# Two-queue filter loads, duplicated rows and one product on GpSimd in the first batch of a fused spectral-filter and MLP kernel

## The chip, the cores and the metric

The kernel runs on one core of one Trainium2 chip. The metric is the device time of one execution in microseconds (us), median of several. Engines are named as in the profile: PE is TensorE, DVE is VectorE, ACT is ScalarE, POOL is GpSimd, SP is SyncE. SP does little but issue transfers here. Moments such as "16.08" are us from the start of the profiled span.

## The reference

Each of 8 sequences of 3008 x 256 goes through a real FFT along the sequence, is multiplied by a complex filter and transformed back; then each of the 24064 tokens goes through a two-layer MLP with a gated activation.

```python
X = np.fft.rfft(x, axis=1)
F = (filt_r + 1j * filt_i)[None, :, :]
y = np.fft.irfft(X * F, n=x.shape[1], axis=1)
h = y.reshape(24064, 256) @ w_in                      # 256 x 2048
out = (h * (1.0 / (1.0 + np.exp(-beta * h)))) @ w_out  # 2048 x 256
```

## The kernel before

The MLP of one batch runs on PE for about 100 us, and the transform of the next batch is slipped between its matmuls by a fixed plan of steps. Only the first batch's transform stands alone, at the start, with the loads of the constants beside it. The change concerns that stretch.

The spectrum lies in six *units* of four rows each (24 rows, `KU = 4`). For each unit, PE makes a bank `sps`, DVE multiplies it by the real and by the imaginary filter (`fr_sb`, `fi_sb`: 128 partitions x 24 x 256 float32), and PE transforms the two products back. Both filters are needed on all 128 partitions, but the two halves hold the same values. So each is loaded to one half only, in a forward and a mirrored piece (the mirrored one reads its rows backwards, in packets of 1 KB), and POOL copies it to the other half ("spread").

```python
    def load_filters(k0, k1):
        n = k1 - k0
        for filt, dst, p0 in ((filt_r, fr_sb, M), (filt_i, fi_sb, 0)):
            for q0, off, sg in ((p0, k0, 1), (p0 + H, N1 - k0, -1)):
                src = AP(filt.tensor, filt.offset + off * D, [[N1 * D, H], [sg * D, n], [1, D]])
                nc.sync.dma_start(dst[q0 : q0 + H, k0:k1, :], src)
    # ... cut ...
    for u in range(NUN):
        load_filters(u * KU, (u + 1) * KU)      # 24 loads of 128 KB on SP's hardware queue
    # ... cut ...
    p0pool = rpool("p0pool", r_p0, bufs=2, **tw)
    def s2_0(u):
        ps = bank2([P, KU, D])
        # ... four matmuls into ps; pq[u, 0], pq[u, 1] = tiles of p0pool, two buffers each ...
        nc.vector.tensor_tensor(pq[u, 0][:], ps[:], fr_sb[:, ks, :], ALU.mult)
        nc.vector.scalar_tensor_tensor(pq[u, 1][:], ps[:], rot[:], fi_sb[:, ks, :], ALU.mult, ALU.mult)
    # ... unit(u): PE transforms pq[u, 0] and pq[u, 1] back, ACT empties the bank ...
    def spread(u):
        ks = slice(u * KU, (u + 1) * KU)
        nc.gpsimd.tensor_copy(fr_sb[:M, ks, :], fr_sb[M:, ks, :])
        nc.gpsimd.tensor_copy(fi_sb[M:, ks, :], fi_sb[:M, ks, :])
    # ... order on POOL: spread(0..3), win load, spread(4), win load, spread(5), x of batch 1 ...
```

Of the kernel before, what the change touches and what calls it, by code (L numbers as in the profile page):

```python
# [22 lines left out]
M = 64  # L23
# [13 lines left out]
def kernel(  # L37
# [48 lines left out]
    def load_filters(k0, k1):  # L86
        n = k1 - k0
        for filt, dst, p0 in ((filt_r, fr_sb, M), (filt_i, fi_sb, 0)):
            for q0, off, sg in ((p0, k0, 1), (p0 + H, N1 - k0, -1)):
                src = AP(filt.tensor, filt.offset + off * D, [[N1 * D, H], [sg * D, n], [1, D]])  # L90
                nc.sync.dma_start(dst[q0 : q0 + H, k0:k1, :], src)  # L91
# [49 lines left out]
    def iota(tile_, pattern, base=0, ch=0):  # L141
        nc.gpsimd.iota(tile_, pattern=pattern, base=base, channel_multiplier=ch)
# [42 lines left out]
    iota(vi[:, :, :H], [[1, NK], [N1, H]])  # L185
    load_x0(16, 24)
    iota(vi[:, :, H:], [[1, NK], [-N1, H]], base=N1 * (M - 1))
# [31 lines left out]
    v_i = shift_and("v_i", 5, 1)  # L219
    q_p = (affine("q0", q_i, -1.0, 1.0), affine("q1", q_i, 1.0, 0.0))  # L220

    def t2_half(hi):
        t = sq.tile([P, NK, H], I32, name="u", tag=f"u{hi}")
        nc.vector.tensor_scalar(  # L224
            t[:], vi[:, :, hi * H : (hi + 1) * H], ms[:], off[:], ALU.mult, ALU.add
        )
        fold(t[:])
        nc.scalar.activation(
            t2[:, :, hi * H : (hi + 1) * H], t[:], ACT.Sin, scale=TWO_PI / TURN
        )  # L230

    def t2_shift(hi):
        for c in range(2):
            d0, s0 = (0, M) if c == 0 else (M, 0)
            dst = t2[d0 : d0 + M, :, M + hi * H : M + (hi + 1) * H]
            src = t2[s0 : s0 + M, :, hi * H : (hi + 1) * H]
            if c == hi:
                nc.vector.tensor_scalar_mul(dst, src, -1.0)
            else:
                nc.vector.tensor_copy(dst, src)  # L240
# [26 lines left out]
    def spin(n, idle):  # L267
        for _ in range(n):
            nc.tensor.matmul(idle[:], lhsT=rest[:, :P], rhs=rest[:], start=True, stop=True)
# [41 lines left out]
    for u in range(NUN):  # L311
        load_filters(u * KU, (u + 1) * KU)
    gp = nc.gpsimd
    rot = affine("rot", v_i, 2.0, -1.0, gp)
# [3 lines left out]
    gp.tensor_tensor(beta_sb[:], tiny[:], beta_sb[:], ALU.add)  # L318
    s1_0(0, (False,))
    s1_0(1, (True,))  # L320
    spin(5, idle)
    t2_shift(0)
    t2_shift(1)
# [102 lines left out]
    def s2_0(u):  # L426
        ps = bank2([P, KU, D])
        for i in range(KU):
            k1 = u * KU + i
            nc.tensor.matmul(ps[:, i, :], lhsT=t2[:, k1, :], rhs=a0[:, k1, :], start=True, stop=True)  # L430
        ks = slice(u * KU, (u + 1) * KU)
        for c in range(2):
            pq[u, c] = p0pool.tile([P, KU, D], BF16, name="pq_t", tag=f"pq{c}")
        nc.vector.tensor_tensor(pq[u, 0][:], ps[:], fr_sb[:, ks, :], ALU.mult)
        nc.vector.scalar_tensor_tensor(
            pq[u, 1][:], ps[:], rot[:], fi_sb[:, ks, :], ALU.mult, ALU.mult
        )
# [45 lines left out]
    spread(4)  # L483
    load_win(4 * P, FF)
    spread(5)
    for g in range(4):
        load_x(1, g)
    load_wout(0)
    load_wout(WG)
    scale_wout(0)  # L490
    scale_wout(WG)
# [8 lines left out]
    s2_0(2)  # L500
    unit(1)
    a0_turn(4)
    s2_0(3)
    unit(2)
    s2_0(4)
    a0_turn(5)
    t3_part(2, True)
    t3_neg(2, True)
    unit(3)
    s2_0(5)  # L510
    idle = tpsum.tile([P, 512], F32, name="tps", tag="tps")
    spin(3, idle)
    unit(4)
# [158 lines left out]
    for b in range(1, B):  # L672
        o = first_step[b - 1]
        if b == 1:
            at(0, z_late, 1, 0)
            at(1, z_late, 1, 1)
            s1_steps(1, range(16), [1 + (2 * i + 1) // 3 for i in range(16)], False, (1, 4, 7, 10, 13))
            for i, r in enumerate((11, 12, 13, 14)):
                at(r, f_late, 1, i // 2, i % 2)
            for g in range(NG):  # L680
                at(o + 13, a2_load, 1, g)
# [147 lines left out]
```

## Time and profile before

| | before |
|---|---|
| time, median (range) | 782.4 us (781.73 to 782.9), 4 runs |
| first filter product / third unit's first product | 16.08 / 20.74 |
| last filter product ends | 30.61 |
| first MLP matmul | 33.84 |
| wait for batch 1's x | 0.84 at 36.61 |

The prediction below shows the waits of PE, the windows and the end of the first batch. The timeline of POOL (start, duration, engine, line, operation, in brackets the idle time before it and what ended that):

```profile
13.11 1.03 POOL L472 COPY fr_sb<-fr_sb 64x1024 f32<-64x1024 f32 x1 [0.98 <-DMA fr_sb<-in_filt_r_dram]
...
28.23 1.04 POOL L473 COPY fi_sb<-fi_sb 64x1024 f32<-64x1024 f32 x1
29.21 2.06 POOL L171 DMA_DIRECT2D xg<-in_x_dram  x4
```

Twelve copies of about 1.04 us, with two loads of `win` between them, fill most of POOL's time from 13 to 29 us, and x can be issued only behind them. The third unit's first product, in DVE's timeline, waits for nothing:

```profile
20.74 1.21 DVE L434 TENSOR_TENSOR pq_t<-sps,fr_sb 128x1024 bf16<-128x1024 f32 x1
```

Then the DMA issues (size of one, median us from issue to landing):

```profile
fr_sb<-in_filt_r_dram SPq DMA_DIRECT2D x12, 128.0 KB, 4.4
fi_sb<-in_filt_i_dram SPq DMA_DIRECT2D x12, 128.0 KB, 4.4
```

They go out on one queue, unit by unit, real and imaginary in turn, which is the order in which DVE needs them.

### The profile page before, as it was taken

Reading aid. Unit: us, or ns where it says so; the run is one execution under the profiler, and the core shown is the slowest. Engines: PE = TensorE matmul, PEld = TensorE weight load, DVE = VectorE, ACT = ScalarE, POOL = GpSimd, SP = SyncE. Lnnn points to the kernel's source line nnn. Section 1 sums busy time; section 2 is a strip of 40 time slices with the busy share of each in tenths; the row PEclk is TensorE's granted clock in tenths of the full one; section 3 lists DMA queues with packets and bytes.
Section 4 is the critical chain, followed back from the end, with each engine's and each line's share of the span. In section 5 each row is a group of like instructions: output and inputs, shape, how many; then the busy total and the mean of one; then the engine's idle time right before and its main releaser. Section 6 shows DMA issues by size and latency. Waiting matters only on the chain.

```text
span 780.2 us, 15154 instructions
## 1 busy us (share of the span) xinstructions
PE 764.1 (98%) x5956; PEld 544.0 (70%) x6051; DVE 446.0 (57%) x713; ACT 552.6 (71%) x814; POOL 151.4 (19%) x155
## 2 busy tenths in 40 slices
PE   8899999999999999999999999999999999999997
PEld 5677667766776667866678666776667776676665
DVE  7869754766556665566546665567655666321001
ACT  6767877676677766777667776677766777777776
POOL 6714400312012210122201322022200222000000
PEclk9999999999999999999999999999999999999999
DMA  9975585244913358042671417622164111500101
GB/s 185 233 213 116 147 209 155 70 108 115 252 42 80 103 116 242 29 113 71 152 207 45 119 48 181 176 75 69 48 189 135 48 48 49 156 28 28 55 28 55
DMA packets 84411, 88.51 MB, mean 113 GB/s; under 512 B 5788, under 2 KB 74652, under 8 KB 84340
## 3 DMA queue, kind: packets, MB, share of 16 engines
q1 hardware_dynamic: 79892, 73.81, 32.0%
q0 software_dynamic: 4304, 13.60, 10.5%
q8 instruction: 47, 0.77, 0.4%
q14 instruction: 24, 0.20, 0.1%
q10 hardware_dynamic: 144, 0.13, 0.0%
HBM read 54.47 MB, written 46.66 MB: 130 GB/s over the span
## 4 chain that ended last, share of the span: by engine, by line
PE 94%; DMA 2%; issue 1%; POOL 1%; DVE 1%; SPq 0%; ACT 0%; DVEq 0%; POOLq 0%
PE acc L788 43%; PE hps L770 39%; PE ps L561 3%; PE ps L629 3%; PE ps L607 3%; PE ps L577 2%; DMA xg<-in_x_dram 1%; DMA fi_sb<-in_filt_i_dram 1%; POOL fi_sb L473 0%; POOL fr_sb L472 0%; SPq L91 0%; PE ps L405 0%; PE tp L400 0%; DVE y L114 0%; DVE u L224 0%
## 5 line engine op out<-in xcount | busy, mean ns | idle before, releaser
L779 ACT ACTIVATE gT<-hps,beta_sb 128x512 bf16<-128x512 f32 x752 | 516.9, 687 | 213.3 <-PE hps L770 191.9
L788 PE MATMUL acc<-wout_sb,gT 128*128 128x256 bf16 x3008 | 452.9, 272 | 2.3
L770 PE MATMUL hps<-y,win_sb 128*128 128x512 bf16 (+7 forms) x1636 | 428.0, 350 | 0.1
L788 PEld LDWEIGHTS <-gT 128*128 128x128 bf16 x3008 | 286.9, 98 | 121.6 <-issue 0.9
L596 POOL TENSOR_TENSOR yh<-a_t,b_t 128x512 bf16<-128x512 f32 x84 | 106.4, 1267 | 424.1 <-DVE b_t L595 422.8
L770 PEld LDWEIGHTS <-win_sb 128*128 128x128 bf16 x1728 | 164.8, 98 | 25.2 <-issue 0.9
L112 DVE COPY ost<-acc 128x512 f32<-128x512 f32 (+1 forms) x94 | 59.9, 679 | 138.3 <-PE acc L788 138.2
L112 DVE CAST a<-ps 96x512 bf16<-96x512 f32 x107 | 72.9, 685 | 53.3 <-PE ps L561 49.3
L114 DVE TENSOR_SCALAR y<-ps 128x376 bf16<-128x376 f32 (+2 forms) x128 | 63.3, 510 | 61.2 <-PE ps L629 57.9
L591 DVE TENSOR_TENSOR a_t<-ps,fr_sb 128x512 f32<-128x512 f32 x84 | 58.1, 692 | 67.0 <-PE ps L577 66.5
L592 DVE SCALAR_TENSOR_TENSOR b_t<-ps,fi_sb 64x512 f32<-64x512 f32 x84 | 58.2, 693 | 1.1
L595 DVE TENSOR_TENSOR b_t<-ps,fi_sb 64x512 f32<-64x512 f32 x84 | 57.4, 683 | 1.1
L112 DVE CAST z<-ps 128x512 bf16<-128x512 f32 x72 | 49.3, 684 | 1.7 <-PE ps L607 0.8
L629 PEld LDWEIGHTS <-zz 96*128 96x128 bf16 x448 | 29.7, 97 | 22.9
L561 PE MATMUL ps<-xg,t 94*96 94x512 bf16 x112 | 41.9, 381 | 1.5 <-DMA xg<-in_x_dram 0.8
L629 PE MATMUL ps<-t,zz 96*128 96x94 bf16 x448 | 34.7, 205 | 0.7
L607 PE MATMUL ps<-yh,t 128*128 128x256 bf16 x168 | 32.1, 273 | 0.6
L577 PE MATMUL ps<-a,t 128*128 128x256 bf16 x168 | 32.1, 273 | 0.3
L607 PEld LDWEIGHTS <-t 128*128 128x128 bf16 x168 | 16.2, 98 | 17.7 <-issue 0.7
L577 PEld LDWEIGHTS <-t 128*128 128x128 bf16 x168 | 16.1, 98 | 16.3
L171 POOL DMA_DIRECT2D xg<-in_x_dram x24 | 12.5, 521 | 56.7 <-PE ps L561 56.7
L561 PEld LDWEIGHTS <-t 94*96 94x96 bf16 x112 | 13.8, 123 | 10.3
(95 smaller groups left out, 177.3 us busy)
## 6 DMA issues: line engine op xcount, KB each, us to landing
out_dram<-ost SPq DMA_DIRECT2D x42, 512.0 KB, 3.0
d<-a SPq DMA_DIRECT2D x28, 384.0 KB, 5.1
a<-d SPq DMA_DIRECT2D x28, 384.0 KB, 4.9
d<-z SPq DMA_DIRECT2D x28, 384.0 KB, 3.9
zz<-d SPq DMA_DIRECT2D x28, 384.0 KB, 7.1
xg<-in_x_dram POOLq DMA_DIRECT2D x24, 384.0 KB, 6.3
out_dram<-ost SPq DMA_DIRECT2D x9, 256.0 KB, 3.8
ws<-in_moe_w_out_dram SPq DMA_DIRECT2D x4, 512.0 KB, 6.6
```

Source lines behind the costliest of these rows:

```text
L112: nc.vector.tensor_copy(dst, src)
L114: nc.vector.tensor_scalar_mul(dst, src, scale)
L561: nc.tensor.matmul(ps[:KP], lhsT=t1[:], rhs=xg[b, g][:NP, jj : jj + 2, :], start=True, stop=True)
L577: nc.tensor.matmul(ps[:, e, :], lhsT=t2[:, k0 + e, :], rhs=st["a2", b, g][:, kk + e, :], start=True, stop=True,)
L591: nc.vector.tensor_tensor(a_t[:], ps[:], fr_sb[:, ks, :], ALU.mult)
L592: nc.vector.scalar_tensor_tensor(b_t[:M], ps[M:], -1.0, fi_sb[M:, ks, :], ALU.mult, ALU.mult)
L596: nc.gpsimd.tensor_tensor(yh[:], a_t[:], b_t[:], ALU.add)
L607: nc.tensor.matmul(ps[:, e, :], lhsT=t3[:, 2 * i + e, :P], rhs=yh[:, e, :], start=True, stop=True)
L629: nc.tensor.matmul(ps[:, e, :NP], lhsT=zz[:, j0 % JG + e, dc * P : (dc + 1) * P], rhs=t4[:], start=True, stop=True,)
L770: nc.tensor.matmul(hps[:, pos - t0 : pos - t0 + ln], lhsT=win_sb[:, dc, fb * P : (fb + 1) * P], rhs=ys[b][:, dc, n0 : n0 + ln], start=(dc ...
L779: nc.scalar.activation(gT[:], hps[:], ACT.Silu, scale=beta_sb[:, fb : fb + 1])
L788: nc.tensor.matmul(acc_of(i, tb)[:, tb % 2, :], lhsT=blk[i * NFB + fb][:, tb * P : (tb + 1) * P], rhs=wout_sb[:, fb, :], start=(fb == 0 an ...
```

## The change

The intent is to free POOL and DVE. The imaginary filter goes through POOL's software queue, so that two queues load the two halves of the partitions side by side. The rows of units 4 and 5 are loaded to both halves, so that four of the twelve copies go. One of the twelve products moves to POOL (ACT first copies the scaled bank to `zc`). Forward and mirrored pieces go to alternating partitions, so that the setup of `t2` needs two shift operations on DVE instead of four. Batch 1's x is meant to be issued earlier, and its first product comes one MLP step later; some late pieces of batch 0 move from steps 11 to 14 to steps 2 to 5.

```diff
-    for u in range(NUN):
-        load_filters(u * KU, (u + 1) * KU)
+    for k0, k1 in ((0, KU), (KU, KH), (KH, DUP), (DUP, NK)):
+        load_filter(0, k0, k1, M, nc.sync)
+    for i, p0 in enumerate((0, M)):
+        load_filter(i, DUP, NK, p0, nc.sync)          # the duplicates, DUP = 16
...
+    for k0, k1 in ((0, KU), (KU, KH), (KH, DUP), (DUP, NK)):
+        load_filter(1, k0, k1, 0, nc.gpsimd)
... load_filter: each piece to every other partition
-                nc.sync.dma_start(dst[q0 : q0 + H, k0:k1, :], src)
+            eng.dma_start(dst[p0 + hi : p0 + M : 2, k0:k1, :], src)
... POOL: spread(0..3), both win loads, one x load, then the product of unit 4
+    def pool_product(u):
+        for i in range(0, KU, 2):
+            k0 = u * KU + i
+            nc.gpsimd.tensor_tensor(
+                pq[u, 1][:, i : i + 2, :], zc[:, i : i + 2, :], fi_sb[:, k0 : k0 + 2, :], ALU.mult
+            )
... order of the units (cut)
-    s2_0(4)
-    ...
-    unit(3)
-    s2_0(5)
+    s2_0(4, True)
+    pool_product(4)
+    unit(2)
+    ...
+    s2_0(5)
+    unit(3)
     unit(4)
... plan
-            s1_steps(1, range(16), [1 + (2 * i + 1) // 3 for i in range(16)], False, (1, 4, 7, 10, 13))
-            for i, r in enumerate((11, 12, 13, 14)):
+            s1_steps(1, range(16), [2 + (2 * i + 1) // 3 for i in range(16)], False, (1, 4, 7, 10, 13))
+            for i, r in enumerate((2, 3, 4, 5)):
```

More of the change, by code (lines that the diff above doesn't have):

```diff
@@ L84, with load_filter @@
     CH = M * J
-    def load_filters(k0, k1):
-        n = k1 - k0
-        for filt, dst, p0 in ((filt_r, fr_sb, M), (filt_i, fi_sb, 0)):
-            for q0, off, sg in ((p0, k0, 1), (p0 + H, N1 - k0, -1)):
-                src = AP(filt.tensor, filt.offset + off * D, [[N1 * D, H], [sg * D, n], [1, D]])
-                nc.sync.dma_start(dst[q0 : q0 + H, k0:k1, :], src)
+    FILTERS = ((filt_r, fr_sb), (filt_i, fi_sb))
+    DUP = 2 * KH
+    def load_filter(i, k0, k1, p0, eng):
+        filt, dst = FILTERS[i]
+        for hi, off, sg in ((0, k0, 1), (1, N1 - k0, -1)):
+            src = AP(filt.tensor, filt.offset + off * D, [[N1 * D, H], [sg * D, k1 - k0], [1, D]])
+            eng.dma_start(dst[p0 + hi : p0 + M : 2, k0:k1, :], src)
     t1 = consts.tile([NP, KP], BF16, name="t1", tag="t1")
@@ L184 @@
     load_x0(8, 16)
-    iota(vi[:, :, :H], [[1, NK], [N1, H]])
+    viv = vi[:].rearrange("p k (m h) -> p k m h", h=2)
+    iota(viv[:, :, :, 0], [[1, NK], [N1, H]])
     load_x0(16, 24)
-    iota(vi[:, :, H:], [[1, NK], [-N1, H]], base=N1 * (M - 1))
+    iota(viv[:, :, :, 1], [[1, NK], [-N1, H]], base=N1 * (M - 1))
     load_x0(24, 28)
@@ L218 @@
     q_i = shift_and("q_i", 0, 1)
-    v_i = shift_and("v_i", 5, 1)
     q_p = (affine("q0", q_i, -1.0, 1.0), affine("q1", q_i, 1.0, 0.0))
@@ L224, in t2_half @@
         nc.vector.tensor_scalar(
-            t[:], vi[:, :, hi * H : (hi + 1) * H], ms[:], off[:], ALU.mult, ALU.add
+            t[:], viv[:, :, :, hi], ms[:], off[:], ALU.mult, ALU.add
         )
@@ L228, in t2_half, with t2_shift @@
         nc.scalar.activation(
-            t2[:, :, hi * H : (hi + 1) * H], t[:], ACT.Sin, scale=TWO_PI / TURN
-        )
-    def t2_shift(hi):
-        for c in range(2):
+            t2[:, :, :M].rearrange("p k (m h) -> p k m h", h=2)[:, :, :, hi],
+            t[:],
+            ACT.Sin,
+            scale=TWO_PI / TURN
+        )
+    def t2_shift():
+        pairs = t2[:].rearrange("p k m -> p (k m)").bitcast(I32).rearrange("p (k m) -> p k m", k=NK)
+        for c, bit in enumerate((1 << 15, -(1 << 31))):
             d0, s0 = (0, M) if c == 0 else (M, 0)
-            dst = t2[d0 : d0 + M, :, M + hi * H : M + (hi + 1) * H]
-            src = t2[s0 : s0 + M, :, hi * H : (hi + 1) * H]
-            if c == hi:
-                nc.vector.tensor_scalar_mul(dst, src, -1.0)
-            else:
-                nc.vector.tensor_copy(dst, src)
+            nc.vector.tensor_scalar(
+                pairs[d0 : d0 + M, :, H:], pairs[s0 : s0 + M, :, :H], bit, None, ALU.bitwise_xor
+            )
     MG = 4
@@ L310 @@
     nc.sync.dma_start(seen[:], t2[:1, 1, M - 2 : M])
-    for u in range(NUN):
-        load_filters(u * KU, (u + 1) * KU)
+    for k0, k1 in ((0, KU), (KU, KH), (KH, DUP), (DUP, NK)):
+        load_filter(0, k0, k1, M, nc.sync)
+    for i, p0 in enumerate((0, M)):
+        load_filter(i, DUP, NK, p0, nc.sync)
     gp = nc.gpsimd
-    rot = affine("rot", v_i, 2.0, -1.0, gp)
+    rot = affine("rot", q_i, 2.0, -1.0, gp)
     tiny = sp.tile([P, NFB], F32, name="tiny", tag="tiny")
@@ L321 @@
     spin(5, idle)
-    t2_shift(0)
-    t2_shift(1)
+    t2_shift()
     nc.vector.memset(t2[:, 0, M : P : M - 1], 0.0)
@@ L424, with s2_0 @@
     p0pool = rpool("p0pool", r_p0, bufs=2, **tw)
-    def s2_0(u):
+    zc = sr.tile([P, KU, D], F32, name="zc", tag="zc")
+    def s2_0(u, on_pool=False):
         ps = bank2([P, KU, D])
@@ L433, in s2_0 @@
             pq[u, c] = p0pool.tile([P, KU, D], BF16, name="pq_t", tag=f"pq{c}")
+        if on_pool:
+            nc.scalar.activation(zc[:], ps[:], ACT.Copy, scale=rot[:])
         nc.vector.tensor_tensor(pq[u, 0][:], ps[:], fr_sb[:, ks, :], ALU.mult)
+        if on_pool:
+            return
         nc.vector.scalar_tensor_tensor(
@@ L482 @@
     load_win(0, 4 * P)
-    spread(4)
     load_win(4 * P, FF)
-    spread(5)
-    for g in range(4):
-        load_x(1, g)
+    load_x(1, 0)
+    def pool_product(u):
[3 more added lines that the diff above has]
+                pq[u, 1][:, i : i + 2, :], zc[:, i : i + 2, :], fi_sb[:, k0 : k0 + 2, :], ALU.mult
+            )
     load_wout(0)
     load_wout(WG)
-    scale_wout(0)
-    scale_wout(WG)
     s2_0(0)
@@ L500 @@
     s2_0(2)
+    a0_turn(4)
     unit(1)
-    a0_turn(4)
     s2_0(3)
+    a0_turn(5)
+    s2_0(4, True)
+    pool_product(4)
+    for g in range(1, 4):
+        load_x(1, g)
+    scale_wout(0)
+    scale_wout(WG)
     unit(2)
-    s2_0(4)
-    a0_turn(5)
     t3_part(2, True)
     t3_neg(2, True)
-    unit(3)
     s2_0(5)
@@ L676 @@
             at(1, z_late, 1, 1)
-            s1_steps(1, range(16), [1 + (2 * i + 1) // 3 for i in range(16)], False, (1, 4, 7, 10, 13))
-            for i, r in enumerate((11, 12, 13, 14)):
+            s1_steps(1, range(16), [2 + (2 * i + 1) // 3 for i in range(16)], False, (1, 4, 7, 10, 13))
+            for i, r in enumerate((2, 3, 4, 5)):
                 at(r, f_late, 1, i // 2, i % 2)
             for g in range(NG):
-                at(o + 13, a2_load, 1, g)
+                at(o + 14, a2_load, 1, g)
             for hh, z0, f0 in ((2, (13, 14), (15, 16, 17, 18)), (3, (18, 19), (20, 21, 22, 23))):
```

## The prediction

> **What bounds the kernel now.** I read the page first (busy shares, slices, chain), then the waits of TensorE (PE) alone, then windows of 2 us over the first 36 us, then the timeline there.
>
> ```profile
> PE 764.1 (98%) x5956; PEld 544.0 (70%) x6051; DVE 446.0 (57%) x713; ACT 552.6 (71%) x814; POOL 151.4 (19%) x155
> PE   8899999999999999999999999999999999999997
> DMA  9975585244913358042671417622164111500101
> ```
>
> PE is busy nearly everywhere. Only the first two slices (2 x 19.5 us), where the first batch is transformed, are below nine tenths, and there the DMA engines are full. The change touches only these. The waits of PE over the whole run say the same:
>
> ```profile
> PE sps L444 <- ACT y L110: 1.6, 3, 1.1
> ...
> PE ps L561 <- DMA xg<-in_x_dram: 0.8, 1, 0.8
> PE lp L444 <- DVE pq_t L435: 0.6, 1, 0.6
> PE sps L444 <- DVE pq_t L435: 0.5, 1, 0.5
> ```
>
> Columns: who waited for whom, us in total, times, longest. All listed waits of PE come to 6.0 us and lie before 37 us; afterwards it works through a fixed list. So a microsecond gained before 37 us is a microsecond at the end, and there is little more to gain than what follows.
>
> ```profile
> 22.00:24.00 2.00, 1.77 (x24) 1.39 (x22) 2.00 (x2) 1.61 (x3) 1.94 (x3) 1.00 0.99 245
> 24.00:26.00 2.00, 2.00 (x36) 1.89 (x34) 2.00 (x3) 2.00 (x3) 1.89 (x3) 1.00 1.07 250
> ```
>
> Windows (columns PE, weight load, DVE, ACT, POOL busy, clock, DMA share, GB/s): between 16 and 30 us VectorE (DVE) does the twelve filter products without a pause, GpSimd (POOL) is full of the copies that spread the filters to the other 64 partitions, and DMA is full at 226 to 250 GB/s. Three things are balanced, and the timeline shows in what order they let go:
>
> ```profile
> 28.20 1.22 DVE L434 TENSOR_TENSOR pq_t<-sps,fr_sb 128x1024 bf16<-128x1024 f32 x1 [0.41 <-POOL fr_sb L472]
> 29.34 1.27 DVE L435 SCALAR_TENSOR_TENSOR pq_t<-sps,rot,fi_sb 128x1024 bf16<-128x1024 f32 x1
> 31.11 0.66 ACT L110 ACTIVATE y<-lp 128x128 bf16<-128x128 f32 x2 [0.66 <-PE lp L444]
> ...
> 36.61 0.38 PE L561 MATMUL ps<-xg,t 94*96 94x512 bf16 x1 [0.84 <-DMA xg<-in_x_dram]
> ```
>
> The first products start at 16.08, and from start to start two take 2.32 us per unit of four rows. Only the sixth unit waits for its spread copy. Its last product ends at 30.61; ScalarE (ACT) empties the last bank at 31.11, and the MLP's matmuls begin at 33.84. At 36.61 PE waits 0.84 us more for the second batch's x, which POOL could issue only at 29.21, behind the spread copies. That is the chain on the page: filter, spread, spread, x.
>
> [...] filter loads, each to one half, run at 226 to 250 GB/s, while 42 to 44 us, with full-height tiles, shows 378. [...] the 128x512 sum takes 1267 ns on POOL, the 128x512 product 692 on DVE. [...]
>
> **The change part by part.**
>
> *Queues.* The imaginary filter moves from SP to POOL: 8 issues. By interpolation between the 96-run loads (0.52 to 0.69 us) and the 256-run ones (0.72 and 0.84) I take 0.58 each as an estimate, 4.6 us. POOL was idle from 8.56 to 11.66, so this ends near 13.3; the small scaling of t4 (0.47 us) ends near 14.0. The first spread (13.11 before) starts near 14.1 and both of unit 0 end near 16.2. DVE needs them at 16.08 and 17.22: no loss, about 1 us of margin.
>
> *Bytes.* Units 4 and 5 are loaded to both halves: four loads of 256 KB, 1.05 MB on top of 3.15 MB. At the old 230 GB/s the 4.2 MB would take 18.3 us from about 10 us, to 28; if the two queues really fill both halves, say 300 GB/s (my estimate, between 230 and 378), they take 14 us; the duplicates come last, on one queue, so near 230. Then the real duplicate is there at about 24.3 and the imaginary one at about 26[...]. DVE wants the first at 25.4, POOL the second about then.
>
> *Spread.* Four of twelve copies go (4 x 1.04 = 4.2 us of POOL). Eight at a pitch of 1.1 us end near 23; two win loads (0.84, 0.72) and the first x load (0.54) go out by 25, against 29.75. The sixth unit's wait for its copy goes: 0.5 us of DVE.
>
> *The product on POOL.* DVE loses one of twelve products: 1.19 us start to start. ACT gains a scaled copy of 128x1024, 1.02 us. POOL gains two products of 128x512, 2 x 1.27 = 2.5 us, beginning at 25 to 26 when the imaginary duplicate lands, ending at 27.6 to 28.6.
>
> *Sum on DVE.* 1.19 + 0.5 = 1.7 us: last product ends at 28.9. But not all of it reaches PE. ACT was nearly full, and now does in a row from 19.2: three bank copies and two unit copies, the new copy (24.0), unit 2 (25.0), t3 and its negative (26.0, 27.0), unit 3 (about 28), unit 4 (about 29), and only then the last unit at about 29.9 to 30.2. Against 31.11 that is 0.9 to 1.2 us, and this, not 1.7, is what the MLP's start gains: 33.84 becomes about 32.8.
>
> *x and the plan.* The second batch's first product moves from MLP step 1 to step 2, so 0.43 us of PE work comes before it, and the x load is issued 4 us earlier. It does not land 4 us earlier: the POOL queue's packets ran without a gap from 27 us to its landing at 36.56, the win loads first. The estimate is 35.0 to 36. Without the wait PE would want it at about 35.1. So between 0.3 and 0.84 us of the old wait goes. The late quarter units move from steps 11 to 14 to steps 2 to 5: same work, DVE there goes from about 60% to about 90% busy (0.61 us more per step of 1.4), which three banks should absorb; I take 0.1 us off for it.
>
> [...]
>
> Sum: 1.1 (MLP starts earlier) + 0.6 (x) - 0.1 - 0.1 = **1.5 us**. 782.44 - 1.5 = **780.9 us**.
>
> **The rivals.** *The bytes take the place of the copies.* If two queues give no more than one[...], the imaginary duplicate lands near 29, the product on POOL ends near 31.5, unit 4 and the last unit follow it, and the kernel is slower by about 0.5 to 1 us (783.2). For it: DMA is already full from 6 to 42 us, and 1.05 MB is added. Against it: [...]the rate of 378 shows that the engines are not the limit. I give it about one chance in six. *Everything lands:* if ACT keeps up (its copies overlap by 0.1 us each) and x is there on time, the gain is 1.7 + 0.84 less the 0.1 of the late units = 2.4 us: 780.0. *POOL becomes the bound:* its queue now holds 8 issues, 8 copies, 3 issues and the products in one line; 1 us lost early (for example by waiting for the semaphores of the x loads, which land as late as 11.93[...]) delays the first spread or the last product by about as much: gain 0.5, 781.9. *Nothing:* the load of x is hidden behind the same queue and ACT eats the rest: 782.4.
>
> **Range and chances.** The rivals stand at 780.0, 781.9, 782.4 and 783.2, my sum at 780.9; runs of one kernel spread 1.2 us. I take 779.5 to 782.7. To be faster by over 2% it would have to save 15.6 us, more than twice all waits of PE; to be slower by that, a stage of 30 us would have to lose half its length. Chances: 0.005, 0.985, 0.01.
>
> **What would show it.** Right: first product near 16.1, DVE's eleven products without a pause, the last ending near 28.9, the two POOL products near 25.5 to 28; the filter window over 280 GB/s; first MLP matmul near 32.8; the wait for xg under 0.5 us; PE without waits afterwards. Wrong: a DMA wait for fi_sb before the POOL product or the last DVE product, a wait of ps for DVE at steps 2 to 5, or a first product after 16.5. Where the MLP's start gains over 1.5 us, my ACT limit was the false step.

Passages are cut from it, marked where they stood, because no trace or run of this case shows what they said of the hardware: general rules about halves of the partitions, two queues and POOL's part in its loads, of which the numbers from the trace are left or given here; in the rivals, two grounds that leaned on such rules and an example of how POOL could lose time; the lag from the last packet to the landing (for three loads of x the traces show 0.3 to 0.5 us from the start of the last packet: 11.45 to 11.93 and 36.26 to 36.56 before, 40.03 to 40.34 after); and the paragraph on the setup. Loads issued by POOL take it 0.51 to 0.84 us each in the trace before. The sum came to 1.1 + 0.6 - 0.1 - 0.1 = 1.5 us; its last term, 0.1 for the setup, has lost its ground with that paragraph, and without the term the sum is 1.6 us, which is 780.8. The profiles show what the setup did: DVE's operations with the strided input took 1.15 and 0.66 us in both kernels, its shift operations 1.11 us instead of 1.42, and ACT's two with the strided output 1.07 us each instead of 0.84.

## The result and the profile after

The changed kernel takes **784.82 us** (784.5 to 785.17, 4 runs) where the kernel before took 782.4 in the same rounds: ratio 1.0032, 95% interval 1.0014 to 1.0049. Within 2% it is the same, as predicted, but it is slower, not faster, and lies above the predicted range. Ratios here and below are the mean time of one kernel's runs over that of the other's runs in the same rounds, so they are not quite the ratio of the medians quoted.

The two lines of the page that answer to those of before:

```profile
PE   8699999999999999999999999999999999999997
DMA  9976586234832349033580416712164211500101
```

Only the second slice of PE lost (from 8 to 6 tenths); all is decided before 39 us, as expected. The waits of PE, where the wait for xg is gone and other waits stand:

```profile
PE sps L456 <- DVE pq_t L444: 2.4, 2, 1.2
PE sps L438 <- DVE pq_t L447: 2.1, 2, 1.7
...
PE sps L456 <- POOL pq_t L501: 0.9, 1, 0.9
```

Windows of the stretch that was full before (columns as in the prediction):

```profile
22.00:24.00 2.00, 0.72 (x10) 0.45 (x8) 2.00 (x2) 1.66 (x2) 1.01 (x1) 1.00 1.09 217
24.00:26.00 2.00, 1.50 (x20) 1.29 (x20) 1.22 (x2) 0.92 (x1) 1.87 (x2) 1.00 1.11 221
```

PE and POOL have idle time in both windows and DVE in the second, yet the DMA share is full in both. DVE, POOL and PE all wait for loads, directly or through one another. The timeline of DVE shows where:

```profile
17.68 1.23 DVE L444 TENSOR_TENSOR pq_t<-sps,fr_sb 128x1024 bf16<-128x1024 f32 x1 [1.98 <-POOL fr_sb L484]
...
21.95 1.22 DVE L444 TENSOR_TENSOR pq_t<-sps,fr_sb 128x1024 bf16<-128x1024 f32 x1 [1.86 <-POOL fr_sb L484]
...
25.14 1.22 DVE L444 TENSOR_TENSOR pq_t<-sps,fr_sb 128x1024 bf16<-128x1024 f32 x1 [0.78 <-POOL fr_sb L484]
...
31.68 1.22 DVE L444 TENSOR_TENSOR pq_t<-sps,fr_sb 128x1024 bf16<-128x1024 f32 x1 [0.67 <-PE sps L456]
```

The first three units each wait for the copy of their **real** filter, and by the third unit DVE is 4.4 us late (25.14 against 20.74). The timeline of POOL says that those copies wait for the loads:

```profile
16.61 1.03 POOL L484 COPY fr_sb<-fr_sb 64x1024 f32<-64x1024 f32 x1 [2.78 <-DMA fr_sb<-in_filt_r_dram]
...
31.26 2.50 POOL L501 TENSOR_TENSOR pq_t<-zc,fi_sb 128x512 bf16<-128x512 f32 x2 [0.84 <-ACT t L112]
```

The second line also shows how a releaser can mislead. It names ACT, but in the record of the semaphores the instruction waits for the second piece of the imaginary duplicate, which lands at 31.09. Finally PE, where the MLP begins:

```profile
33.81 0.51 PE L456 MATMUL sps<-t,pq_t 128*128 128x128 bf16 x6 [0.94 <-POOL pq_t L501]
...
38.27 0.59 PE L790 MATMUL hps<-y,win_sb 128*128 128x512 bf16 x2 [0.32 <-ACT y L112]
...
40.46 0.38 PE L581 MATMUL ps<-xg,t 94*96 94x512 bf16 x1
```

The MLP starts at 38.27, 4.43 us later than before. Step for step it gets 1.2 us back by step 2, because nothing waits for x now, gives some of that up while DVE is loaded with the late pieces, and from step 15 to the last stays 3.43 us behind. The medians differ by only 2.4: in the one profile of the kernel before, the end of the span after the last step is 0.7 us longer than in that of the changed one. No experiment here says why, so the sections below compare the starts of the MLP and the medians, not single spans.

The DMA issues show the new order of the loads:

```profile
fr_sb<-in_filt_r_dram SPq DMA_DIRECT2D x6, 256.0 KB, 11.5
fi_sb<-in_filt_i_dram POOLq DMA_DIRECT2D x4, 256.0 KB, 7.9
fi_sb<-in_filt_i_dram POOLq DMA_DIRECT2D x4, 128.0 KB, 4.1
```

POOL issued all eight imaginary loads between 8.5 and 13.4. Those of the last two units landed at 20.40 and 22.90, while the last real rows of the second unit came only at 20.76 and those of the third at 23.95.

### The profile page after: what moved, and what is told of

The parts are those of the page before. It is cut to its first block, busy times and chain, and to the rows that moved or that the text cites. A ratio compares the mean times of both kernels' runs of the same rounds, so it can differ in the third digit from the quotient of the medians. Undisturbed runs are those within 1.5% of the kernel's fastest.

```text
span 782.9 us, 15136 instructions
## 1 busy us (share of the span) xinstructions
PE 764.2 (98%) x5955; PEld 544.0 (69%) x6051; DVE 444.8 (57%) x709; ACT 553.8 (71%) x815; POOL 154.6 (20%) x161
## 4 chain that ended last, share of the span: by engine, by line
PE 94%; DMA 1%; issue 1%; DVE 1%; ACT 1%; POOL 1%; SPq 0%; DVEq 0%; POOLq 0%; ACTq 0%
PE acc L808 43%; PE hps L790 39%; PE ps L581 3%; PE ps L649 3%; PE ps L627 3%; PE ps L597 2%; DMA fr_sb<-in_filt_r_dram 1%; SPq L93 0%; PE tp L406 0%; ACT y L112 0%; POOL pq_t L501 0%; PE ps L411 0%; DVE u L226 0%; DVE u L147 0%; DVE pq_t L447 0%
```

## The experiments

I set out with four suspicions, none of them tested by a run at that point; the expectations use these letters. **Q**: the imaginary rows of late units, on the second queue, take bandwidth from the real rows that are needed first. **P**, a form of Q: the queues take turns by packets, so that the hardware queue with its 1 KB packets loses. **B**: the 1.05 MB of duplicates cannot land before 31 (31.09 in the changed kernel) and hold up POOL's product. **S**: loads to every other partition are issued slowly on the hardware queue. "Wrong" marks kernels whose result is wrong because some rows read other rows' filters; their instructions have the same shapes. Two clauses are cut from the expectations, marked: in e1 a lag of the landing, so that the step from 27.9 to "29 to 30" is the author's estimate, and in e8 a cost of issuing.

| run | time | before, same rounds | ratio (95% interval) | MLP start |
|---|---|---|---|---|
| changed kernel | 784.82 | 782.4 | 1.0032 (1.0014 to 1.0049) | 38.27 |
| e1 one queue | 789.89 | 781.86 | 1.0103 (1.0089 to 1.0117) | 41.32 |
| e3 interleaved rows alone | 786.28 | 781.86 | 1.0063 (1.0050 to 1.0076) | 38.37 |
| e4 plan alone | 781.43 | 781.86 | 0.9996 (0.9982 to 1.0009) | 34.01 |
| e5 no duplicates | 784.23 | 781.86 | 1.0029 (1.0016 to 1.0042) | 37.50 |
| e6 two queues alone | 783.26 | 782.13 | 1.0014 (1.0000 to 1.0027) | 36.94 |
| e7 contiguous rows | 784.61 | 782.13 | 1.0033 (1.0020 to 1.0045) | 38.13 |
| e8 small packets | 784.88 | 782.13 | 1.0035 (1.0022 to 1.0047) | 38.40 |
| e9 loads as before | 781.62 | 782.36 | 0.9990 (0.9978 to 1.0003) | 33.53 |
| e10 big packets | 784.35 | 782.36 | 1.0029 (1.0016 to 1.0041) | 39.11 |
| e11 shift alone | 781.57 | 782.36 | 0.9992 (0.9978 to 1.0005) | 34.02 |
| e12 in step with need | 790.16 | 782.36 | 1.0100 (1.0084 to 1.0115) | 43.17 |
| e13 in step, no duplicates | 786.59 | 782.36 | 1.0048 (1.0035 to 1.0061) | 39.00 |
| e14 in order of need | 786.24 | 781.99 | 1.0051 (1.0035 to 1.0067) | 39.36 |
| e15 in order, no duplicates | 780.50 | 781.99 | 0.9978 (0.9960 to 0.9997) | 33.60 |
| e16 in order, plain | 781.99 | 782.31 | 0.9994 (0.9982 to 1.0006) | 34.92 |

One caution for this table: in the first 43 us the profiles of e1, e3, e5, e7, e10, e12, e13 and e14 have TensorE at a granted clock of 0.50 for 3.4 to 10.2 us in all; the other profiles don't. Part of what these eight lose is therefore clock and not the loads directly, and no experiment separates the two. For that reason the ends of the products on DVE and POOL are set beside the times further down.

### e1: the changed kernel on one queue

```diff
-        load_filter(0, k0, k1, M, nc.sync)      # and fi on nc.gpsimd
+        for i, p0 in enumerate((M, 0)):
+            load_filter(i, k0, k1, p0, nc.sync)
```

> The changed kernel, but all filter loads on the one hardware queue, real and imaginary of each range in turn, the duplicates last; nothing goes through the software queue. Theory Q (the two queues at once let the imaginary filter of late units take bandwidth from the real filter of the first units): the first product goes back from 17.7 to about 16.1 us, the three waits of VectorE for spread copies (1.98, 1.86, 0.78) go, and the MLP's first matmul comes before 35; time about 781.5. Theory B (the 1.05 MB of duplicates set the end): the last duplicate still lands at 29 to 30 (4.2 MB at 230 GB/s from 9.6 us is 27.9[...]), the product on GpSimd starts there, MLP start near 36.5 to 37, time about 783.3, although the first product is early.

With the old order the first product starts at 16.26 again, so interleaved rows on one queue do not delay it (e7 will show that two queues with contiguous rows do not either). But the loads now run at 198 GB/s (12 to 20 us; 234 before the change), and POOL's product waits even longer:

```profile
32.85 2.48 POOL L500 TENSOR_TENSOR pq_t<-zc,fi_sb 128x512 bf16<-128x512 f32 x2 [4.32 <-DMA fi_sb<-in_filt_i_dram]
```

So two queues are not simply worse: they brought 257 GB/s in that window.

### e3: interleaved rows alone

```diff
-                nc.sync.dma_start(dst[q0 : q0 + H, k0:k1, :], src)
+            eng.dma_start(dst[p0 + hi : p0 + M : 2, k0:k1, :], src)   # in the kernel before, one queue, no duplicates
```

> The kernel before with one part of the change alone: filter rows on every other partition (and the tables t2, rot and vi that go with it), still one queue, four rows a load, all copies. Theory I (rows on every other partition are written more slowly): 1 KB packets take over 75 ns where the kernel before shows 61 to 71, the last filter lands after 27.5 instead of 26.7, and the time is 783 to 784. Theories Q and B: nothing changes, 782.2 to 782.7.

It costs 0.6%, more than the whole change does. Part of that is the clock (0.50 from 31.0 to 37.9): the last filter product ends 3.4 us later than before, the MLP starts 4.5 later. SP's issues take 0.60 to 0.66 us each instead of 0.31 to 0.43. One queue with one load of 128 KB per 0.655 us moves at most 200 GB/s, and the windows show 180. The packets themselves are quick (1 KB in 46 ns in the median of 12 to 26 us, against 64 before), so it is the issue that limits; the slower packets that I had expected are not there. S is real on one queue.

### e4: the plan alone

```diff
-   [1 + (2 * i + 1) // 3 for i in range(16)]    (11, 12, 13, 14)    at(o + 13, a2_load, 1, g)
+   [2 + (2 * i + 1) // 3 for i in range(16)]    (2, 3, 4, 5)        at(o + 14, a2_load, 1, g)
```

> The kernel before with one part alone: the plan of the MLP steps (second batch's first stage one step later, late quarters at steps 2 to 5 instead of 11 to 14, its loads one step later). Setup unchanged, so MLP start at 33.84. If the plan is what recovered 1.0 us in the changed kernel, the wait of 0.84 for x at 36.6 shrinks to under 0.45, and the time is 781.5 to 782.0. If the recovery came only because the MLP started late there, the time stays at 782.3 to 782.6, or is worse by 0.2 through waits for VectorE at steps 2 to 5.

The same within the interval. Step by step it is 1.05 us ahead at step 2, and most of that is gone by step 10 (0.15), with DVE loaded by the late pieces in between. But where the kernel before has those pieces to do, it gains again, and from step 14 on it stays 0.61 ahead. e11 tries the shift alone, to see whether the late pieces cost the 0.44 that is not regained.

### e5: no duplicate bytes (wrong)

```diff
-    for i, p0 in enumerate((0, M)):
-        load_filter(i, DUP, NK, p0, nc.sync)
...
+        v = u if u < 4 else u - 2      # units 4 and 5 read the filters of 2 and 3
```

> The changed kernel without the four duplicate loads; units 4 and 5 (and the same rows in later batches) read the filters of units 2 and 3 instead, so the result is wrong on purpose. Everything else, queues and order, is as changed. Theory B: the last filter lands near 26.3 instead of 31.1, the product on GpSimd starts when the scaled copy is there (29.4) instead of 31.26, MLP start near 36.4, time about 783.0. Theory Q alone: the first product stays at 17.7 and the third unit's at 25.1, and if these set the end the MLP start stays near 38 and the time near 784.6.

A quarter of the bytes gone, and only 0.6 us won (784.23 against 784.82, different rounds). The early delay is all there (first product 18.39, third unit 25.32). B alone is not the cause. (In this profile the clock is at 0.50 from 20.2 to 23.6 us.)

### e6: two queues alone

```diff
-        load_filters(u * KU, (u + 1) * KU)
+        load_filter(0, u * KU, (u + 1) * KU, M, nc.sync)
...
+    for k0, k1 in ((0, KU), (KU, KH), (KH, DUP), (DUP, NK)):
+        load_filter(1, k0, k1, 0, nc.gpsimd)      # in the kernel before; contiguous, no duplicates
```

> The kernel before (contiguous halves, no duplicates, all copies, all products on VectorE) with one part of the change alone: the imaginary filter goes through GpSimd's queue in eight loads, the real one stays on the hardware queue. The imaginary rows that follow one another come in packets of 4 and 8 KB there, the mirrored real rows in 1 KB packets. Theory P (the two queues take turns by packet, so the queue with larger packets gets more bytes, and the real filter, needed first, falls behind): the real loads of units 0 and 1 land later than in the kernel before (12.94 and 16.66), first product at 17 or later, VectorE waits for copies of fr_sb, time 783.3 to 784.5. If instead two queues simply fill both halves: last filter lands before 25 instead of 26.7, first product 16.1, time 781.3 to 782.

Nothing but the second queue, and the third unit's first product slips from 20.74 to 23.30:

```profile
23.30 1.23 DVE L439 TENSOR_TENSOR pq_t<-sps,fr_sb 128x1024 bf16<-128x1024 f32 x1 [2.50 <-POOL fr_sb L477]
```

The loads move 266 GB/s between 12 and 20 us instead of 234, and the kernel is still 1.1 us slower by the medians (the interval reaches down to 1.0000). More bytes per us, in the wrong order.

### e7: the changed kernel with contiguous rows

```diff
-            eng.dma_start(dst[p0 + hi : p0 + M : 2, k0:k1, :], src)
+            q0 = p0 + hi * H
+            eng.dma_start(dst[q0 : q0 + H, k0:k1, :], src)
```

> The changed kernel with its rows back in contiguous halves of 32 partitions (and the tables that go with it); two queues, duplicates, product on GpSimd and plan as changed. Theory S (a hardware-queue load to every other partition takes its queue 0.60 to 0.66 us to issue instead of 0.31 to 0.43, as run e3_interleave shows, where the transfers are no longer full): issues go back under 0.45. If that is what made the change slower, first product before 16.6, time under 782.5. If transfers, not issues, are the limit in the changed kernel (there they are full, 1 KB packets 53 to 88 ns), first product stays at 17.2 to 17.8 and the time at 784.2 to 784.9.

The first product is back at 15.88, but the third unit's stays at 24.83 and the time at 784.61. S, together with the second queue, explains the first unit's delay and nothing of the result.

### e8: small packets on both queues (wrong, inconclusive)

```diff
+            if back and sg == 1:
+                off, sg = k1 - 1, -1      # imaginary forward rows read backwards
```

> The changed kernel with the imaginary filter's forward rows read backwards, so that they too travel in 1 KB packets instead of 4 and 8 KB; the same bytes, places and number of loads, wrong result on purpose[...]. Theory P: the real filter gets a larger share; its unit 0 lands by 14.5 instead of 16.44 and unit 1 by 17.5 instead of 20.76, first product at 16.1 to 16.6, the waits of VectorE for fr_sb in units 1 and 2 shrink by over half, but the duplicates still land at 30.5 to 31.5 and hold the GpSimd product, so the MLP starts only 0.3 to 1 us earlier, time 783.8 to 784.6. If P is wrong: first product stays at 17.7.

The intervention failed: the software queue gathered the backward rows into packets of 4096 B all the same. Nothing follows for P from it.

### e9: loads as before (wrong)

```diff
-    for k0, k1 in ((0, KU), (KU, KH), (KH, DUP), (DUP, NK)):
-        load_filter(0, k0, k1, M, nc.sync)       # and the duplicates, and fi on nc.gpsimd
+    for u in range(NUN):
+        for i, p0 in enumerate((M, 0)):
+            load_filter(i, u * KU, (u + 1) * KU, p0, nc.sync)
```

> The changed kernel's order, product on GpSimd and plan, but all filter loads as before the change (one queue, four contiguous rows, real and imaginary in turn), no duplicates: the fifth and sixth unit read the third's and fourth's filters, so the result is wrong on purpose. It takes every load term out of the comparison. If the loads alone are what the prediction got wrong, the rest of its sum holds: first product near 16.1, product on GpSimd begun before 27, MLP start at 32.8 to 33.2, no wait for x, a time 1.0 to 1.6 us below the kernel before (ratio 0.998 to 0.9988). If the changed order itself costs (the sixth unit's first product now waits for the fourth unit's matmuls, for want of a third buffer, and ScalarE's row of copies is longer), the MLP starts at 34 or later, and the ratio is 1.000 or above.

The MLP starts at 33.53, which is 4.7 us earlier than in the changed kernel: the loads are what went wrong. But it is only 0.3 earlier than before the change, where 1.1 was predicted. The line of DVE for the sixth unit shows why:

```profile
27.62 1.22 DVE L443 TENSOR_TENSOR pq_t<-sps,fr_sb 128x1024 bf16<-128x1024 f32 x1 [1.00 <-PE sps L455]
```

The products have two buffers each. The new order puts `s2_0(5)` ahead of `unit(3)`, so this product must wait until PE has read the fourth unit's. The prediction did not have that step. The wait for x is not gone either (1.10 us), so the gain of 0.7 us by the medians, in an interval that includes 1, is about half of what I expected.

### e10: big packets for the real rows (wrong)

```diff
+            if i == 0 and sg == -1:
+                off, sg = N1 - k1 + 1, 1      # the real mirrored rows read forwards
```

> The changed kernel with the real filter's mirrored rows read forwards, so that the hardware queue too sends packets of 4 KB and more where it sent 1 KB; the same bytes from nearly the same addresses, a wrong result on purpose. If the queues take turns by packets, so that the one with large packets gets more bytes, the first real unit lands by 14.5 instead of 16.4, the second by 17.5 instead of 20.8, and the first product starts by 16.6 instead of 17.7. If the delay comes only from sharing one total rate, or from the slow issue of interleaved rows, these move by less than 0.7 us. In both cases the duplicates still end near 30 to 31, the MLP starts only 0.3 to 1.0 us earlier, and the time is 784.0 to 784.6.

The first real unit lands at 14.86 instead of 16.44, the second at 17.79 instead of 20.76, the first product starts at 16.30: the size of their packets did shift the landings of these loads, by 1.6 and 3.0 us, as P had it. That the queues take turns by packets is not shown by this. The third unit's rows still land only at 23.27 (23.95 before this edit), and the time falls by no more than rounds differ. The MLP even starts later, at 39.11. PE now idles in one piece, and after that it runs slowly:

```profile
26.93 1.04 PE L440 MATMUL sps<-a,t 128*128 128x256 bf16 x4 [3.97 <-DVE pq_t L449]
```

Four such matmuls take 0.60 us elsewhere. The windows give a granted clock of 0.95 from 24 to 26 us and of 0.50 from 26 to 32: in the 3.97 us without a matmul the clock falls to 0.50, 2.9 us after the last one ended. (The profiled run was the slowest of this kernel's five.)

### e11: the shift alone

```diff
-   [1 + (2 * i + 1) // 3 for i in range(16)]    at(o + 13, a2_load, 1, g)
+   [2 + (2 * i + 1) // 3 for i in range(16)]    at(o + 14, a2_load, 1, g)
```

> The kernel before with one thing of the change alone: the second batch's first product moved from MLP step 1 to step 2 (and the load that follows its last sum one step later); the late quarters stay at steps 11 to 14. The run with the whole plan showed the wait for x gone, with 1.05 us won by step 2, but about 0.4 us given back between steps 2 and 15. If the late quarters at steps 2 to 5 gave it back, this kernel keeps 0.7 to 0.9 us: 781.0 to 781.4 where the kernel before has 782.1, ratio 0.9988 to 0.9992. If the shift itself gives it back, it is the same within 0.3 us.

As expected in the median (0.8 us down), though the interval includes 1. The wait for x, 0.84 before, is still 0.47. By the trace this kernel is 1.05 us ahead at step 2 like e4, but from step 12 on only 0.19, where e4 stays 0.61 ahead. So on balance the late pieces were not what gave the gain back, as the expectation supposed, and the medians of e4 and e11 do not tell the two apart.

### e12 and e13: the imaginary loads in step with need, with and without duplicates

```diff
-    for k0, k1 in ((0, KU), (KU, KH), (KH, DUP), (DUP, NK)):
+    for k0, k1 in ((0, KU), (KU, KH)):
         load_filter(1, k0, k1, 0, nc.gpsimd)
...  spread(u):
+        if u == 0:
+            load_filter(1, KH, DUP, 0, nc.gpsimd)     # between the two copies of unit 0
...  after spread(3):
+    load_filter(1, DUP, NK, 0, nc.gpsimd)
```

> The changed kernel with contiguous rows, both queues and the duplicates kept, but the imaginary filter's loads in step with need: before the first spread GpSimd issues only units 0 and 1, the third and fourth unit after the first copy, the last two after the last copy; the real filter goes four rows at a time. The result stays correct. If the imaginary rows of late units were taking the bandwidth from the real rows needed first, the third unit's real filter lands by 18.5 instead of 23.6 (contiguous rows), its first product starts by 21.5 instead of 24.8, and DVE's first eight products run nearly without a pause. The total of bytes is unchanged, so the imaginary duplicate still lands at 29.5 to 31.5 and GpSimd's product begins then: the MLP starts at 37.0 to 38.2, and the time is 783.5 to 784.5. If something else held the third unit up, its product stays at 24 or later.

> The kernel in step with need, and without the duplicates (the fifth and sixth unit read the third's and fourth's filters, a wrong result on purpose). Both delays are taken away together, on two queues. If the two delays in parallel are the whole cause, the MLP starts at 33.3 to 34.0, as in the run with the loads of before (33.53), and the time is within 0.5 us of that run's (781.6): 1.5 to 3 us below the run with the duplicates alone removed (784.23). If two queues cost something by themselves, the MLP starts at 35 or later and the time is 783 or more.

Both expectations on the time fell badly. The half that concerned Q held: in e12 the third unit's real rows land by 18.09 and its real product starts at 20.96. But its imaginary copy then waits 5.56 us for the loads issued at 15.1 and 15.7 (timeline of POOL in e12):

```profile
26.25 1.04 POOL L489 COPY fi_sb<-fi_sb 64x1024 f32<-64x1024 f32 x1 [5.56 <-DMA fi_sb<-in_filt_i_dram]
```

In the trace, the first of these two loads' packets starts at 20.36. For 4.6 us after the end of its issue the software queue moved nothing, while the hardware queue worked off, at 171 to 254 GB/s, what it had been given before. Set beside each other, the loads of both queues landed in the order in which they were issued:

```
issued   queue      rows                          landed
14.9     hardware   real duplicate, forward       23.78
15.1     software   imaginary units 2, 3 forward  24.52
15.7     software   imaginary units 2, 3 mirrored 26.12
16.0     hardware   real duplicate, mirrored      26.85
```

So the picture behind Q and P was itself incomplete. To a first order the loads land as if **served in the order of issue, whatever their queue**. It is no more than a first order: in e15 two software loads issued at 15.52 and 16.05 landed at 24.00 and 25.12, before a hardware load in 1 KB packets issued at 14.39 (25.95), and in e10 the packet sizes shifted landings by 1.6 and 3.0 us. What I had meant to bring in step I had put at the end of a line. The 4.6 us without a packet don't agree with P's turns by packets for loads issued into such a backlog.

In e13 the same copy waits 4.81 us, so its MLP starts at 39.00 although the duplicates are gone. The long stops also cost clock: in e12 PE idles 6.06 us from 22.60 on and then runs at 0.50 (windows from 26 to 28 and 28 to 30 us). The two runs therefore could not test whether the two delays together are the whole cause. That remained open and was the reason for the next two.

### e14 and e15: loads issued in the order of need, with and without duplicates

```diff
...  against e12; in spread(u), between the two copies:
         if u == 0:
-            load_filter(1, KH, DUP, 0, nc.gpsimd)
+            load_filter(1, DUP, NK, 0, nc.gpsimd)
...
+    load_filter(1, KH, DUP, 0, nc.gpsimd)
     for u in range(4):
         spread(u)
-    load_filter(1, DUP, NK, 0, nc.gpsimd)
```

> The changed kernel with contiguous rows, both queues and the duplicates, its loads issued in the order of need: the real filter four rows at a time; the imaginary rows of the third and fourth unit are issued at about 12.2 to 13.3, after the real rows of the third unit and before the first copy; the last imaginary rows after the first copy. Correct result. If loads are served in the order of issue whatever their queue, the imaginary rows of the third unit land by 21 (they landed at 24.5 to 26.1 when issued at 15.1), DVE's first eight products run from 16 with pauses of under 1 us in all, and the third unit's first product starts by 21.5. The duplicates still land at 28.5 to 31 and GpSimd's product waits for them: MLP start 35.5 to 37.8, time 783.0 to 784.3. If the queues shared by turns instead, the real rows of the third unit would be held up by the imaginary ones and its product would start at 22.5 or later.

> The same without the duplicates; the fifth and sixth unit read the third's and fourth's filters, a wrong result on purpose. Neither of the two named delays is left. If they are the whole cause, the MLP starts at 33.3 to 34.3 (33.53 with the loads of before), and the time is 781.2 to 782.4, ratio 0.998 to 1.0003: that is 2 to 3 us below the run that had only the duplicates removed (784.23). If the MLP starts at 35 or later although no product waits for a load or a copy before 26, there is a third cause.

In both, DVE goes through the first eight products from 16 to 26.5 with pauses of 0.7 to 0.9 us in all, and the third unit's real product starts at 21.05 and 21.28. Order of issue is confirmed as the lever. (These two also load the real filter four rows at a time instead of eight. That alone is not it: e6 does the same with the imaginary filter issued at once, and the last real piece of the third unit, issued at 11.63, lands at 22.10; in e14 it is issued at 11.67 and lands at 18.50.) In e14 the work then waits for the duplicates: DVE for the real one, which is there at 28.57, POOL for the imaginary one, at 31.10 as in the changed kernel:

```profile
31.27 2.49 POOL L506 TENSOR_TENSOR pq_t<-zc,fi_sb 128x512 bf16<-128x512 f32 x2 [4.25 <-DMA fi_sb<-in_filt_i_dram]
```

That this comes out even slower than the changed kernel (786.24) is again the clock, by the window after PE's three waits of 1.2, 2.0 and 0.9 us, with 0.6 and 0.3 us of work between them:

```profile
34.00:36.00 2.00, 2.00 (x22) 1.91 (x19) 0.00 (x0) 1.24 (x3) 2.00 (x4) 0.51 1.12 226
```

The sixteen matmuls of the last unit take 1.91 us there and 1.06 in the changed kernel. In e15 no product of the third unit or later waits for a load or a copy by more than 0.05 us, and the time falls by as much as was predicted, to 780.50 us. The third unit's first product, the product on POOL, and PE's timeline:

```profile
21.28 1.22 DVE L445 TENSOR_TENSOR pq_t<-sps,fr_sb 128x1024 bf16<-128x1024 f32 x1
...
26.71 2.50 POOL L505 TENSOR_TENSOR pq_t<-zc,fi_sb 128x512 bf16<-128x512 f32 x2
...
29.26 0.51 PE L457 MATMUL sps<-t,pq_t 128*128 128x128 bf16 x6 [0.34 <-POOL pq_t L505]
...
33.60 0.59 PE L796 MATMUL hps<-y,win_sb 128*128 128x512 bf16 x2
...
35.79 0.38 PE L585 MATMUL ps<-xg,t 94*96 94x512 bf16 x1
```

Four kernels now form a square:

| | duplicates | no duplicates |
|---|---|---|
| imaginary filter issued at once | 784.61 (e7) | 784.23 (e5) |
| issued in the order of need | 786.24 (e14) | 780.50 (e15) |

Taking away one delay alone wins 0.4 us or loses 1.6; taking away both wins 4.1. The delays lie side by side, and whichever is left sets the end. (e5 has interleaved rows, the others contiguous ones; with duplicates that makes 0.2 us, e7 against the changed kernel. Without duplicates it was not tried. The lower row also has the four-row loads.) The times of e14, e7 and e5 have the clock in them, so look at the ends of the products too, DVE's last and POOL's: 34.10 and 33.76 in the changed kernel, 34.27 and 33.16 in e5, 32.50 and 33.76 in e14, 30.38 and 29.21 in e15. With the order of need alone POOL's end does not move, without the duplicates alone DVE's does not, and with both gone both come some 4 us earlier.

### e16: what is left, in a correct kernel

```diff
-        load_filters(u * KU, (u + 1) * KU)      # kernel before, with the shift of e11
+    for u in range(4):
+        load_filter(0, u * KU, (u + 1) * KU, M, nc.sync)
+    for u in range(4, NUN):
+        for i, p0 in enumerate((M, 0)):
+            load_filter(i, u * KU, (u + 1) * KU, p0, nc.sync)
...
+    for u in range(2):
+        load_filter(1, u * KU, (u + 1) * KU, 0, nc.gpsimd)
... ahead of the first copy
+    load_filter(1, KH, DUP, 0, nc.gpsimd)
```

> The kernel before, with three things: the imaginary filter of units 0 to 3 goes through the software queue, issued in the order of need (as in the runs in order), everything else stays on the hardware queue; contiguous rows; the second batch's first product one MLP step later. No duplicates, no product on GpSimd, a correct result. The spread copies can run 1 to 1.5 us earlier than before the change, so the sixth unit's wait (0.5) goes and the x load goes out about 1 us earlier: last product at 30.1 to 30.4 (30.61 before), MLP start 33.2 to 33.7, wait for x under 0.3, time 780.7 to 781.4, ratio 0.998 to 0.9993. If the six issues cost GpSimd as much as the copies win, it is like the run with the shift alone (0.9992).

It missed: last product at 31.69 instead of 30.4, MLP start 34.92. The sixth unit still waits 0.42 us for its copy and the fifth 0.37, POOL waited 1.28 and 0.67 for loads, and so the copies ended at 30.34 (29.27 before). No wait for x is left. The second queue does not pay here. No kernel with a right result clearly beats the kernel before; the plan alone (e4) and the shift alone (e11) beat the changed kernel and are not worse than the kernel before.

## Why the prediction was wrong

**Right.** The stretch that decides, and within 2%; nothing shifts any more after step 15; PE without lasting waits in the plan; the durations: POOL's eight issues 4.88 us (4.6 predicted), its product 2.50 (2.5), ACT's copy 1.11 (1.02). The rival "the bytes take the place of the copies" named the right mechanism for one of the two delays: it put the imaginary duplicate near 29 and the end of POOL's product at 31.5, and they came at 31.09 and 33.76.

**Right by luck: the wait for x.** It is gone (0.84 before), but not because x was issued 4 us earlier, as the prediction says. It was issued at 29.85 (29.21 before), behind the late copies, and landed at 40.34, just before PE used it at 40.46 in an MLP that was itself 4.4 us late. In e9 x was issued at 25.10, about as predicted; it landed at 36.94, after the 35.0 to 36 estimated, and PE waited 1.10.

**Two loose readings.** Between 16 and 30 us the 2 us windows before the change run from 210 to 328 GB/s, not from 226 to 250. And the windows of 226 to 250 that the prediction sets beside 378, as loads "each to one half", hold loads to both halves, so they do not show what one half takes.

**The step that failed first: "Bytes".** The prediction took 300 GB/s for two queues, "(my estimate, between 230 and 378)", and so the duplicates at 24.3 and 26. The trace has 257 GB/s between 12 and 20 us and 212 between 22 and 28, when nearly only the hardware queue is at work; the duplicates came at 28.64 and 31.09. Over the 234 of one queue in the same window, 257 is 10% more; the estimate of 300 stood for 28%.

**The second: "Queues".** "The first spread (13.11 before) starts near 14.1 ... no loss, about 1 us of margin" counted POOL's time for the issues and not what they do to the loads beside them. The first spread started at 16.61. By the order of issue, the third unit's real rows were the last of 2.62 MB (all 1.57 of the imaginary filter and their own 1.05), where before 1.57 MB sufficed for both filters of three units. At the rates measured that is 10.2 instead of 6.7 us, by my estimate 3.5 us more; DVE was 4.4 late. e6 shows this delay without the rest (2.6 us), e14 and e15 show it removed. The first unit's share has the interleaved rows in it as well (e7: 15.88 instead of 17.68), an issue cost that the prediction did not foresee and that does not decide.

**The third, smaller: "Sum on DVE".** The sixth unit's first product waits for a buffer (0.67 in the changed kernel, 1.00 in e9), so ACT was not the only limit of the MLP's start.

**The rest of the sum.** Without late loads (e15) the kernel is 1.5 us faster by the medians, which is the 1.5 predicted. Not all of its terms are, though: the MLP's start gains 0.24 instead of 1.1, and from there to step 15 come another 1.0 (1.25 in all) where x and the plan were to bring 0.4. The total agrees partly because these misses cancel, which is luck.

**Not settled.** Why the stretch from the last MLP step to the end of the span is some 0.7 us longer in one profile than in the other. Whether, in the changed kernel itself, the clock costs something: its two runs at 785.01 and 785.17 have a mean clock of 0.997, those at 784.5 and 784.63 one of 1.0, but only one has a trace. Whether the software queue's 4.6 us without a packet in e12 is the backlog alone, or whether something else held its transfers as well: no run issues the same loads with an empty hardware queue. And whether the order of issue holds beyond loads of the sizes here.

## What to carry to other kernels

A second DMA queue was not a second road here (257 to 266 GB/s against 234, 10 to 14% more): before moving loads to one, list all loads of both queues by their moment of issue and add up the bytes ahead of each one that somebody waits for. Loads that were needed late and issued early were paid for by those needed first (in e6 the third unit's first product slips from 20.74 to 23.30), and a load issued late into a backlog waited for most of it (in e12, issued at 15.1 and landed at 24.52). When a kernel is balanced, several delays can lie side by side, so that undoing any one part of a change can show nothing (0.4 us won or 1.6 lost for one delay alone here, 4.1 won for both); undo them together before you acquit one of them.
